# FFT-filter mixing and SwiGLU feed-forward on one core: the filter-half copies, the order and the engine split of the first sequence's prologue

## The chip, the cores and the metric

The kernel runs on one core of a Trainium2 chip. Times are device microseconds (us). "Span" is the time from the first to the last instruction of a profiled execution; it is about 1.8 us shorter than the time of the same run. I quote medians, and ratios with a 95% interval.

The engines are named as in the profile: PE is TensorE (matmuls), DVE is VectorE, ACT is ScalarE, POOL is GpSimd, SP is SyncE, whose queue issues DMAs here.

## The reference, cut to what matters

```python
# x: 8 sequences of 3008 x 256, filt_r and filt_i: 1505 x 256
Y = np.fft.rfft(x, axis=1) * (filt_r + 1j * filt_i)[None]
a = np.fft.irfft(Y, n=3008, axis=1).reshape(24064, 256)
xn = a / np.sqrt(np.mean(a * a, axis=-1, keepdims=True) + 1e-6) * rms_g
g = xn @ w_gate                                     # 256 -> 1536
out = (g / (1 + np.exp(-g)) * (xn @ w_val)) @ w_out # 1536 -> 256
```

The kernel does the transform as matmuls: a first DFT stage ("stage A", tile `pat`), transposes (`pt`), a second stage (the "products", tile `psb`, numbered 0 to 15), a multiplication with the filter, and the way back (`pgt`). Then come the norm and the feed-forward part, whose first matmul is the gate product `pg`.

## The kernel before

Sequence 0 has nothing to overlap with. It is done on chip in a prologue that ends with the first `pg` at about 50 us. After that, TensorE always has feed-forward work of one sequence to mix with the transform of the next.

A filter chunk is loaded into one half of 128 partitions and copied into the other half, because the multiplication needs the real part and the imaginary part on both halves. These are the parts that matter:

```python
def b_unit(b, i):                       # one product unit; b is the sequence
    ps = bank(3 if b else (0, 3, 4, 5)[i % 4], "psb")   # written out in two branches
    for u in range(2):
        ...
        nc.tensor.matmul(ps[:, u, :], w[:, k, :], t, start=True, stop=True)
    ...
    eng = nc.vector
    if (i in (5, 8, 11, 14)) if b else (i in (4, 8, 11)):
        eng = nc.gpsimd                 # ScalarE copies PSUM to v, GpSimd multiplies
        ...
        nc.scalar.activation(out=v, in_=ps, func=AXT.Copy)
    eng.tensor_tensor(out=s1, in0=ps, in1=f1, op=ALU.mult)
    eng.tensor_tensor(out=s2, in0=ps, in1=f2, op=ALU.mult)

def f_dup(c):                           # copy the halves of filter chunk c
    for t, a, e in ((fr[c], HALF, 0), (fi[c], 0, HALF)):
        if c == 2 or (c == 3 and a):
            nc.scalar.activation(out=t[a:a + HALF], in_=t[e:e + HALF], func=AXT.Copy)
        else:
            nc.gpsimd.tensor_copy(out=t[a:a + HALF], in_=t[e:e + HALF])
```

```python
# the prologue's program order, cut
for c in range(4):
    f_load(c, filt_r, fr[c], 0, nc.sync)
    if c < 3:
        f_load(c, filt_i, fi[c], HALF, nc.gpsimd)
nc.sync.dma_start(gsb, moe_rms_g...)    # the 256 gains, one per partition
...
for i in range(8):
    t1_unit(i)                          # transposes, and a copy by VectorE or ScalarE
f_dup(0); f_load(3, filt_i, ...); f_dup(1)
for i in range(16):
    if i == 7: f_dup(3)
    b_unit(0, i)
    if i % 2 and i >= 5: bit_unit(i - 5); bit_unit(i - 4)
    if i == 4: f_dup(2)
    if i == 11: w_load(0); w_load(1)    # the feed-forward weights
```

## Time and profile before

| | before |
|---|---|
| median of the first 3 runs | 904.32 us |
| profiled span | 903.3 us |
| TensorE busy | 878.7 us, 97% |
| last part of x on chip (last DMA engine) | 15.5 us |
| transposes start | 17.1 us |
| VectorE's filter products | 22.5 to 41.5 us |
| first gate product | 50.6 us |

The head of the profile's page gives the span, then busy time, share of the span and instruction count of each engine:

```profile
span 903.3 us, 17520 instructions
...
PE 878.7 (97%) x6329; PEld 561.0 (62%) x6329; DVE 676.9 (75%) x1075; ACT 619.3 (69%) x1047; POOL 391.4 (43%) x353
```

TensorE bounds the kernel as a whole, but it is not busy all through the prologue. The windows view shows this; each line is one stretch of the prologue, with busy time and instruction count of each engine, then the granted TensorE clock, the DMA share and GB/s:

```profile
core 0: us, PE busy (x) PEld busy (x) DVE busy (x) ACT busy (x) POOL busy (x), PEclk, DMA share, GB/s
...
17.00:34.00 17.00, 10.99 (x138) 8.54 (x139) 14.71 (x24) 11.07 (x13) 14.76 (x12) 0.96 0.62 138
34.00:44.00 10.00, 8.60 (x89) 7.54 (x89) 5.53 (x9) 5.60 (x13) 9.37 (x10) 0.55 0.30 48
44.00:52.00 8.00, 5.67 (x53) 3.82 (x53) 3.78 (x9) 3.67 (x7) 4.69 (x7) 0.87 1.20 174
```

From 17 to 34 us VectorE and GpSimd are the busiest engines. From 34 to 44 us TensorE seems to be, but at a granted clock of 0.55: it does little work in a lot of busy time.

VectorE's timeline over the products (start, duration, engine, line, operation, and in brackets the idle time before it and what ended that). Each multiplication takes about 0.68 us, and one follows the other every 0.6 us:

```profile
22.50 0.69 DVE L263 TENSOR_TENSOR ss<-psb,fr 128x512 f16<-128x512 f32 x1
...
32.92 0.68 DVE L264 TENSOR_TENSOR ss<-psb,fi 128x512 f16<-128x512 f32 x1
35.93 0.69 DVE L263 TENSOR_TENSOR ss<-psb,fr 128x512 f16<-128x512 f32 x1 [2.32 <-POOL ss L263]
...
40.80 0.68 DVE L264 TENSOR_TENSOR hh<-psb,fi 128x512 f16<-128x512 f32 x1
```

The stretch lasts 22.50 to 41.48, 19.0 us, and it has one hole of 2.32 us, which waits for a GpSimd product. GpSimd's timeline shows why: that product itself started late, since ScalarE had to bring it its copy `v` and was in two filter copies of 1.9 us:

```profile
34.61 1.26 POOL L263 TENSOR_TENSOR ss<-v,fr 128x512 f16<-128x512 f32 x1 [1.56 <-ACT v L261]
```

TensorE's timeline at the start of the prologue: stage A waits for x, then 64 transposes, then the products. The last line is the first gate product.

```profile
15.66 0.94 PE L486 MATMUL pat<-tb,xc 128*128 128x128 f16 x14 [0.76 <-DMA xc<-in_x_dram]
17.11 4.64 PE L509 MATMUL pt<-tb,aT 128*128 128x128 f16 x64 [0.51 <-ACT aT L492]
22.03 0.38 PE L241 MATMUL psb<-t,wbp 96*128 96x256 f16 x2 [0.28 <-DVE t L511]
...
50.59 1.06 PE L420 MATMUL pg<-xn,wg 128*128 128x512 f16 x2
```

### The profile page before, as it was taken

How to read it: one execution, taken by the hardware profiler on the slowest of the kernel's cores; microseconds unless marked ns; L12 is line 12 of the kernel's file. 1: busy time of each engine (PE TensorE's matmuls, PEld its weight loads, DVE VectorE, ACT ScalarE, POOL GpSimd, SP SyncE). 2: the span in 40 equal slices, each digit the busy share in tenths (PEclk: the TensorE clock that was granted, in tenths of full speed). 3: DMA queues.
4: the chain of work that ended last, by engine and by line, in shares of the span. 5: the costliest groups of instructions: out<-in, count | busy, mean ns of one | idle time of the engine just before them, and what ended most of it. 6: DMA issues, size and time to landing. Idle time of an engine off the chain costs nothing.

```text
span 903.3 us, 17520 instructions
## 1 busy us (share of the span) xinstructions
PE 878.7 (97%) x6329; PEld 561.0 (62%) x6329; DVE 676.9 (75%) x1075; ACT 619.3 (69%) x1047; POOL 391.4 (43%) x353
## 2 busy tenths in 40 slices
PE   8689999999999999999999999999999999999997
PEld 5565666666666666666666666666666666666564
DVE  7756767789887887888788886887878887555554
ACT  8657666677677766877667766787657765676443
POOL 7832740555635552465325552265514552043300
PEclk9799999999999999999999999999999999999999
DMA  9495734774664437444554347243252332321201
GB/s 199 82 182 159 144 76 164 166 171 79 165 168 116 90 72 213 106 95 113 135 147 111 88 96 193 81 105 82 74 173 71 65 88 54 97 70 48 60 24 46
DMA packets 79747, 100.91 MB, mean 112 GB/s; under 512 B 8097, under 2 KB 56417, under 8 KB 79277
## 3 DMA queue, kind: packets, MB, share of 16 engines
q1 hardware_dynamic: 69276, 83.45, 33.8%
q0 software_dynamic: 10384, 16.35, 11.4%
q8 instruction: 49, 0.80, 0.4%
q14 instruction: 38, 0.30, 0.1%
HBM read 67.67 MB, written 46.78 MB: 127 GB/s over the span
## 4 chain that ended last, share of the span: by engine, by line
PE 86%; issue 5%; DMA 3%; DVE 2%; POOL 2%; ACT 2%; SPq 0%; POOLq 0%; ACTq 0%
PE po L437 25%; PE pg L420 25%; PE pv L420 25%; PE psi L286 3%; PE psb L241 3%; PE psn L318 2%; DMA fr<-in_filt_r_dram 2%; PE psa L204 2%; PE psq L339 1%; DVE o L443 1%; DMA rb<-r_tmp 1%; POOL xc L189 0%; DVE hh L425 0%; ACT fr L478 0%; ACT sg L424 0%
## 5 line engine op out<-in xcount | busy, mean ns | idle before, releaser
L425 DVE TENSOR_TENSOR hh<-pv,sg 128x512 f16<-128x512 f32 (+1 forms) x576 | 391.4, 680 | 203.6 <-ACT sg L424 88.9
L424 ACT ACTIVATE sg<-pg 128x512 f16<-128x512 f32 (+1 forms) x576 | 338.8, 588 | 231.1 <-PE pg L420 223.1
L437 PE MATMUL po<-wo,hh 128*128 128x256 f16 x2256 | 342.3, 272 | 2.3 <-DVE o L443 1.6
L420 PE MATMUL pv<-xn,wv 128*128 128x512 f16 (+1 forms) x1152 | 337.9, 375 | 0.0
L420 PE MATMUL pg<-xn,wg 128*128 128x512 f16 (+1 forms) x1152 | 337.9, 375 | 0.0
L437 PEld LDWEIGHTS <-hh 128*128 128x128 f16 x2256 | 216.5, 98 | 99.2 <-issue 3.6
L277 POOL TENSOR_TENSOR s<-s,s 128x512 f16<-128x512 f16 x96 | 110.5, 1151 | 285.5 <-DVE s L271 199.5
L420 PEld LDWEIGHTS <-wv 128*128 128x128 f16 x1152 | 112.7, 98 | 131.2 <-issue 0.6
L403 POOL TENSOR_TENSOR xn<-y,rb 128x1024 f16<-128x1024 f32 (+1 forms) x45 | 126.1, 2802 | 46.7 <-DMA rb<-r_tmp 32.8
L420 PEld LDWEIGHTS <-wg 128*128 128x128 f16 x1152 | 109.2, 98 | 12.3 <-issue 0.3
L345 POOL TENSOR_TENSOR rho<-u,mhalf 128x4 f32<-128x4 f32 (+1 forms) x48 | 48.9, 1018 | 85.6 <-DVE u L343 85.6
L291 ACT ACTIVATE t<-psi 96x512 f16<-96x512 f32 x112 | 66.3, 592 | 11.8 <-PE psi L286 6.3
L324 ACT ACTIVATE y<-psn,gsb 128x512 f32<-128x512 f32 (+1 forms) x94 | 63.8, 678 | 10.1 <-PE psn L318 3.0
L271 DVE TENSOR_TENSOR s<-psb,fi 64x512 f16<-64x512 f32 x96 | 65.7, 684 | 3.0
L273 DVE SCALAR_TENSOR_TENSOR s<-psb,fi 64x512 f16<-64x512 f32 x96 | 66.5, 693 | 1.3
L247 DVE TENSOR_TENSOR s<-psb,fr 128x512 f16<-128x512 f32 x96 | 65.4, 681 | 0.0
L330 ACT ACTIVATE sq<-psn 128x512 f16<-128x512 f32 (+1 forms) x94 | 54.8, 583 | 0.0
L209 ACT ACTIVATE t<-psa 128x512 f16<-128x512 f32 x70 | 41.8, 597 | 5.6 <-PE psa L204 2.4
L286 PE MATMUL psi<-s,wi 128*128 128x256 f16 x248 | 45.4, 273 | 0.0
L241 PE MATMUL psb<-t,wb 96*128 96x256 f16 x224 | 43.0, 272 | 0.9 <-DVE s L264 0.9
L286 PEld LDWEIGHTS <-wi 128*128 128x128 f16 x248 | 24.2, 98 | 27.0 <-issue 1.9
L318 PEld LDWEIGHTS <-t 128*128 128x128 f16 x368 | 28.5, 99 | 19.9
(97 smaller groups left out, 515.7 us busy)
## 6 DMA issues: line engine op xcount, KB each, us to landing
out_dram<-o SPq DMA_DIRECT2D x84, 256.0 KB
xc<-in_x_dram POOLq DMA_DIRECT2D x56, 192.0 KB, 6.4
z_tmp<-t SPq DMA_DIRECT2D x28, 384.0 KB
t<-z_tmp SPq DMA_DIRECT2D x28, 384.0 KB
g_tmp<-t SPq DMA_DIRECT2D x56, 192.0 KB
rb<-r_tmp SPq DMA_DIRECT2D x41, 256.0 KB
t<-g_tmp SPq DMA_DIRECT2D x21, 384.0 KB
out_dram<-o SPq DMA_DIRECT2D x12, 192.0 KB
```

The source lines that it names most:

```text
L241: nc.tensor.matmul(ps[:, u, :], w[:, k, :], t, start=True, stop=True)
L247: nc.vector.tensor_tensor(out=s1, in0=ps, in1=f1, op=ALU.mult)
L271: nc.vector.tensor_tensor(out=s2[a], in0=ps[e], in1=f2[e], op=ALU.mult)
L273: nc.vector.scalar_tensor_tensor(out=s2[a], in0=ps[e], scalar=-1.0, in1=f2[e], op0=ALU.mult, op1=ALU.mult)
L277: nc.gpsimd.tensor_tensor(out=s, in0=s1, in1=s2, op=ALU.add)
L286: nc.tensor.matmul(ps[:, u, :], wi_at(q, 2 * i + u), ss[q][:, u, :], start=(q == 0), stop=(q == n - 1))
L291: nc.scalar.activation(out=st[b]["t3"][c][:, 2 * r:2 * r + 2, :], in_=ps[0:KR], func=AXT.Copy)
L403: nc.gpsimd.tensor_tensor(out=xv, in0=yv, in1=rv.unsqueeze(1).to_broadcast([P, 2, n, P]), op=ALU.mult)
L420: nc.tensor.matmul(ps[:, 0:w], wt[:, dt_, ts(jt, P)], xn[:, dt_, 0:w], start=(dt_ == 0), stop=(dt_ == 1))
L424: nc.scalar.activation(out=sg[:, 0:w], in_=pg[:, 0:w], func=AXT.Silu)
L425: nc.vector.tensor_tensor(out=hh[:, 0:w], in0=pv[:, 0:w], in1=sg[:, 0:w], op=ALU.mult)
L437: nc.tensor.matmul(po[s4 // 2][:, s4 % 2, :], hh[:, ts(s4, P)], wo[:, jt, :], start=(jt == 0 and s4 % 2 == 0), stop=(jt == JT - 1 and (s4 ...
```

## The change

The intent is to shorten VectorE's product stretch and to start it earlier. The filter halves are copied by three hands at once: ScalarE for most real halves, GpSimd for most imaginary ones, a DMA within the on-chip memory for one half. Products 0 to 3 are issued between the first transposes. GpSimd takes four product units instead of three. The load of the gains moves to the head of the SyncE queue, some small work moves between engines, and six warm-up matmuls fill the wait for x.

```diff
-        if (i in (5, 8, 11, 14)) if b else (i in (4, 8, 11)):
+        if (i in (5, 8, 11, 14)) if b else (i in (3, 7, 10, 13)):
# b_unit is split: b_mm issues the matmuls, b_unit can take its result
-    def f_dup(c):
+    def f_dup(c, which=(0, 1)):
+        for e in which:
+            t = (fr, fi)[e][c]
+            a, o = (0, HALF) if e else (HALF, 0)
+            if c == 3 and e == 0:
+                nc.sync.dma_start(t[a:a + HALF], t[o:o + HALF])
+            elif e and c < 3:
+                nc.gpsimd.tensor_copy(out=t[a:a + HALF], in_=t[o:o + HALF])
             else:
+                nc.scalar.activation(out=t[a:a + HALF], in_=t[o:o + HALF], func=AXT.Copy)
# y_first: the second half of the norm's multiply moves from VectorE to ScalarE
# t1_unit: transposes go to the PSUM pools pg and pv; ScalarE copies groups 1, 4 and 6 only
+        nc.sync.dma_start(gsb, moe_rms_g...)          # the gains, now before the filter
         for c in range(4):
             f_load(c, filt_r, fr[c], 0, nc.sync)
-            if c < 3:
-                f_load(c, filt_i, fi[c], HALF, nc.gpsimd)
-        nc.sync.dma_start(gsb, moe_rms_g...)
+            f_load(c, filt_i, fi[c], HALF, nc.gpsimd if c < 3 else nc.sync)
# stage A, before its fifth group:
+            if m == 4:
+                warm_up(6, 0)
-        for i in range(8):
-            t1_unit(i)
+        t1_unit(0)
         f_dup(0)
-        f_load(3, filt_i, fi[3], HALF, nc.gpsimd)
-        f_dup(1)
+        t1_unit(1)
+        ps0 = [b_mm(0, i) for i in range(4)]
+        t1_unit(2)
+        f_dup(3, (0,))
         for i in range(16):
-            b_unit(0, i)
+            b_unit(0, i, ps0[i] if i < 4 else None)
# t1_unit(3..7) and the other f_dup calls now follow units 0 to 10;
# w_load(0) and w_load(1) come after unit 13 instead of 11; t2_unit(2) copies on ScalarE
```

## The prediction

> What bounds the kernel now. Over the whole span the matmul engine is busy 878.7 of 903.3 us (page, part 1), and from 66 us on it is busy 97 to 99% of each stretch (windows view). Nothing in the change touches that part. The change works between 8 and 52 us, before the first gate product (timeline: pg at 50.8 us). A microsecond saved there should come off the end nearly one for one; far less than 2% (18 us) can be saved.
>
> How that prologue runs (timeline and landings in the trace):
> - DMA is saturated from 6 to 31 us. The last part of x lands at 15.5 us; filter chunk 0 at 18.5 (real) and 19.3 (imaginary); the last chunk at 28.8 and 31.0. The change does not lower these bytes (it adds 0.5 MB of copy), so the start of the transposes (17.1 us) stays.
> - VectorE then sets the pace: 13 product units of two 0.68 us multiplications (about 1.2 us a unit, pipelined), from 22.5 to 41.5 us. Pure work is 15.6 us; the main hole is 2.3 us at 33.6 (a wait for a GpSimd product that started late, at 34.6, since ScalarE was in 1.9 us filter copies).
> - TensorE is at half its clock from 32.8 to 43.0 us and from 49.9 to 53.3 (windows view by microsecond: 0.50). There a 96-wide product takes 0.08 instead of 0.043 us, and TensorE is the limit from 37 to 43 us.
>
> What the change does, costed:
> 1. Unit 3, 7, 10, 13 to GpSimd in place of 4, 8, 11: one unit less on VectorE, -1.2 us; the 2.3 us hole should mostly go, since GpSimd no longer copies the real halves (2 x 1.9 us) and ScalarE's imaginary-half copy moves behind the products' start.
> 2. First copies in parallel: real half of chunk 0 on ScalarE 18.6 to 20.5, imaginary on GpSimd 19.4 to 21.3 (before: ready at 22.5).
> 3. That gain is not collected: ScalarE's 1.0 us transpose copy of group 1 now stands behind its 1.9 us filter copy, so TensorE's products 2 and 3 wait until about 21.5, transposes of group 2 follow, and VectorE's copy of group 2 stands before product 0. I expect product 0 at about 23.4, later than before by about 1 us.
> 4. Sum for VectorE from 23.4: 12 x 1.2 + 3 x 0.6 = 16.2 us, plus about 1 us of holes: last product ends near 40.5 (before 41.5).
> 5. After it: one normalization multiply (0.75 us) and one transpose copy (0.4) leave VectorE's chain: 0.5 us saved before the first xn.
> 6. The memset and the six warm-up matmuls hide in the wait for x at 15.5.
>
> Clock: [...] TensorE's new hole at 19 to 21.5 may bring half clock early; fewer holes later may shorten the one at 33 to 43. This is worth 1 to 2 us either way.
>
> Predicted: first gate product at about 48.5 (before 50.8), time 902.0 us, 80% range 899.3 to 904.3. Faster by over 2%: 0.01; within: 0.985; slower: 0.005.
>
> Right if: chain has no 2.3 us GpSimd hole, product 0 starts near 23.4, first gate product comes 1 to 4 us earlier, stretch after it is as long as before. Wrong if: half clock covers 22 to 40 us, the DMA copy of chunk 3's real half lands after 36 us, or work after the prologue waits for x or weights, whose loads don't move.

The forecast came to 2.3 us, from 50.8 to 48.5 us for the first gate product and from 904.3 to 902.0 us in time. The "1 to 2 us either way" for the clock stands outside the sum; it was the author's estimate, and the text does not say from which numbers. What the text calls saturated DMA is a DMA share of 0.95 from 6 to 29 us in the windows view of the kernel before; from 29 to 30 us the share is 0.37, from 30 to 31 us nil.

## The result

| | before | after |
|---|---|---|
| median (4 runs each) | 904.31 us | 904.12 us (903.08 to 905.43) |
| ratio | 1 | 0.9998 (0.998 to 1.0015) |
| profiled span | 903.3 us | 902.2 us |

904.12 lies just within the predicted range, at its upper edge (904.3). The expected 2.3 us did not come: the medians differ by 0.2 us. A change worth nothing would have landed in the range too, so the hit by itself says little about the mechanism.

The head of the page after the change. Totals hardly move:

```profile
span 902.2 us, 17535 instructions
...
PE 875.6 (97%) x6335; PEld 559.0 (62%) x6335; DVE 672.9 (75%) x1070; ACT 622.7 (69%) x1051; POOL 390.3 (43%) x351
```

The windows view after, same stretches and columns as before:

```profile
17.00:34.00 17.00, 10.77 (x128) 9.49 (x128) 10.37 (x18) 10.61 (x10) 9.85 (x8) 0.90 0.77 167
34.00:44.00 10.00, 6.97 (x110) 5.80 (x110) 8.44 (x15) 8.52 (x18) 8.57 (x8) 1.00 0.08 16
44.00:52.00 8.00, 5.07 (x56) 3.46 (x54) 3.42 (x8) 5.16 (x10) 7.11 (x11) 1.00 1.07 158
```

VectorE has 4.3 us less work from 17 to 34 us (10.37 against 14.71) and 2.9 us more from 34 to 44. The clock is now 1.00 from 34 to 52 us, where it was 0.55 and 0.87.

VectorE's timeline after: the product stretch starts 3.7 us later than before, has no hole, and ends only 1.0 us later, at 42.44.

```profile
25.60 0.69 DVE L519 COPY t<-pt 96x1024 f16<-96x1024 f16 x1 [4.26 <-PE pt L517]
26.21 0.68 DVE L264 TENSOR_TENSOR ss<-psb,fr 128x512 f16<-128x512 f32 x1
...
41.76 0.68 DVE L265 TENSOR_TENSOR hh<-psb,fi 128x512 f16<-128x512 f32 x1
```

TensorE's timeline after shows two things that made the start late: x is waited for longer (1.62 us against 0.76), and products 2 and 3 wait 2.22 us for ScalarE's copy `t`.

```profile
18.09 0.94 PE L494 MATMUL pat<-tb,xc 128*128 128x128 f16 x14 [1.62 <-DMA xc<-in_x_dram]
19.54 1.60 PE L517 MATMUL pt<-tb,aT 128*128 128x128 f16 x16 [0.51 <-ACT aT L500]
21.40 0.60 PE L237 MATMUL psb<-t,wbp 96*128 96x256 f16 x4 [0.26 <-DVE t L519]
24.21 0.60 PE L237 MATMUL psb<-t,wbp 96*128 96x256 f16 x4 [2.22 <-ACT t L521]
...
51.05 0.38 PE L424 MATMUL pg<-xn,wg 128*128 128x512 f16 x1 [0.22 <-DVE xn L396]
```

ScalarE's timeline names the cause of the second: the copy `t` that TensorE needs stands behind the filter copy, which waits for the filter to land.

```profile
21.21 1.91 ACT L488 ACTIVATE fr<-fr 64x2048 f32<-64x2048 f32 x1 [1.73 <-DMA fr<-in_filt_r_dram]
23.14 1.02 ACT L521 ACTIVATE t<-pt 96x1024 f16<-96x1024 f16 x1
```

In this trace the first gate product comes at 51.05, not earlier than before (50.59). The span is 1.1 us shorter all the same.

### The profile page after: what moved, and what is told of

Read it like the earlier page. It is cut to its first block, busy times and chain, and to the rows that moved or that the text cites. A ratio compares the mean times of both kernels' runs of the same rounds, so it can differ in the third digit from the quotient of the medians.

```text
span 902.2 us, 17535 instructions
## 1 busy us (share of the span) xinstructions
PE 875.6 (97%) x6335; PEld 559.0 (62%) x6335; DVE 672.9 (75%) x1070; ACT 622.7 (69%) x1051; POOL 390.3 (43%) x351
## 4 chain that ended last, share of the span: by engine, by line
PE 87%; issue 5%; DVE 2%; DMA 2%; POOL 2%; ACT 1%; SPq 0%; DVEq 0%; POOLq 0%; ACTq 0%
PE po L441 25%; PE pg L424 25%; PE pv L424 25%; PE psb L237 3%; PE psi L287 3%; PE psn L319 2%; PE psa L204 2%; DMA fr<-in_filt_r_dram 1%; PE psq L340 1%; DVE o L447 1%; DMA rb<-r_tmp 1%; PE pt L517 0%; POOL xc L189 0%; DVE hh L429 0%; ACT sg L428 0%
## 5 line engine op out<-in xcount | busy, mean ns | idle before, releaser
L346 POOL TENSOR_TENSOR rho<-u,mhalf 128x4 f32<-128x4 f32 (+1 forms) x48 | 48.9, 1018 | 82.4 <-DVE u L344 82.4
```

## The experiments

The questions were these. Does the move of the gains delay x and the filter? Does the position of ScalarE's first filter copy cost the start? What does the clock do? And why does an earlier first gate product not shorten the time?

Twelve kernels were run, in three groups of four. Each group ran on one chip, and its four kernels share the runs of the before kernel. All were timed and all gave correct results. The before kernel's median in the three groups was 905.38, 905.55 and 905.98 us, with 11 runs each. It ranged from 903.9 to 908.1 us in the second group, so one run of one kernel says little about 1 us.

Three readings recur. "Landed" is when 15 of the 16 DMA engines had delivered x; this leaves out one slow engine. "Half clock" is a stretch in which the trace's clock records show a granted clock of 0.5. Half-clock time per run is worked out from the mean granted clock c and the span as 2·(1 − c)·span; figures for a kernel are means over its runs, since c is on record to 0.001, which is 1.8 us of half clock. The before kernel has 18.7 to 20.4 us of it in the three groups. In the fourteen traces 0.7 to 3.6 us of it lies at the very end of the span. The first 4 to 7 us of a trace have no clock record and count as full clock.

### e1: the changed kernel with the gains loaded late again

```diff
-        nc.sync.dma_start(gsb, moe_rms_g...)     # before the filter loads
         for c in range(4):
             f_load(...)
+        nc.sync.dma_start(gsb, moe_rms_g...)     # after them, as in the kernel before
```

> The changed kernel with the load of the 256 gains put back behind the filter loads. Theory A (the 4-byte packets of the gains at the head of the queue delay x and filter chunk 0): x is complete near 15.5 us instead of 17.95, real filter chunk 0 is ready near 18.7 instead of 21.1, product 0 starts near 23.7 instead of 26.2, and the time is about 2 us under the changed kernel (902). Theory B (the late x has another cause: the moved memset, the moved loads, or chance of that run): x still completes after 17 us, product 0 after 25.5, time within 0.7 us of the changed kernel.

Measured: median 906.70 us, ratio 1.0006 (0.9972 to 1.0039). x landed at 15.59 and real filter chunk 0 at 18.63, against 16.5 and 21.11 in the first trace of the changed kernel. The time did not improve. The trace of this run is spoiled for a direct comparison: the DFT tables landed 1.6 us late (8.56 instead of 7.0), and TensorE was at half clock from 9.0 to 19.3 us, so the transposes began only at 22.8. The timed runs are free of that choice of one trace, and they show no gain from this edit alone: theory A's 902 did not come.

### e2: the kernel before with the gains loaded first

```diff
+        nc.sync.dma_start(gsb, moe_rms_g...)
         for c in range(4):
             f_load(...)
-        nc.sync.dma_start(gsb, moe_rms_g...)
```

> The kernel before with nothing changed but the load of the gains moved to the head of the queue. Theory A: x completes near 17.5 to 18 us instead of 15.5, product 0 starts near 25 instead of 22.5, time 2 us over the kernel before (906.5). Theory B: x completes by 16.2 us, time within 0.7 us of the kernel before.

Measured: median 906.21 us, ratio 1.0008 (0.9977 to 1.0039). x landed at 16.25, against 15.0 in the kernel before. As in e1, half clock early on (9.9 to 20.2 us) spoiled the trace, and the DFT tables were late here too (8.39). The direction of the landing is as the theory of the gains says; no loss of time can be told from 1.

### e3: the changed kernel with the filter copy behind the second transposes

```diff
         t1_unit(0)
-        f_dup(0)
         t1_unit(1)
+        f_dup(0)
```

> The changed kernel with the transposes of group 1 and their ScalarE copy placed ahead of the ScalarE copy of filter chunk 0. Theory (the 1.0 us transpose copy behind the 1.9 us filter copy holds TensorE, and through the copy of group 2 VectorE's first product): the 2.2 us wait of the products for that copy vanishes, product 0 starts when the filter copy ends, near 23.2 instead of 26.2, VectorE's last product ends near 40 instead of 42.4, and the time falls by 1 to 2 us (less if GpSimd's last product, which ended at 42.9, then sets the end). Rival (the filter's arrival at 21.1 alone sets the start): product 0 moves by under 1 us, time within 0.5 us.

Measured: median 904.04 us, ratio 0.9976 (0.9946 to 1.0006). TensorE's timeline shows the wait gone, 0.16 us instead of 2.22:

```profile
21.35 1.01 PE L237 MATMUL psb<-t,wbp 96*128 96x256 f16 x4 [0.16 <-ACT t L521]
```

VectorE's first product started at 23.69 and the first gate product at 48.88, 2.2 us earlier than in the changed kernel's first trace. Against its second trace (e6 below: 24.26 and 48.47) the gate product is not earlier, so only the vanished wait is sure. The interval includes 1, so the gain in time is likely but not shown by this run alone.

### e4: both edits, e1 and e3

> Both edits: gains late, and group 1's transposes ahead of the filter copy. If both theories hold: x complete near 15.5, product 0 near 21.4, last product near 38 to 40, first gate product near 47.5 to 49 instead of 51, time 900 to 901.5. If only the copy order counts: about 902.5; if neither: about 904.

Measured: median 904.77 us, ratio 0.9985 (0.9954 to 1.0016); the 900 to 901.5 us expected if both theories hold did not come. TensorE's timeline shows the best start so far: a short wait for x, and none of note for ScalarE.

```profile
16.04 0.94 PE L494 MATMUL pat<-tb,xc 128*128 128x128 f16 x14 [0.32 <-DMA xc<-in_x_dram]
...
20.17 0.60 PE L237 MATMUL psb<-t,wbp 96*128 96x256 f16 x4 [0.23 <-ACT t L521]
```

The first VectorE product starts at 22.12 and the last ends at 38.35, 3.1 us earlier than in the kernel before (41.48). Yet the first gate product is at 48.87 and the span at 903.2. So 3 us in the middle of the prologue gave 1.7 us at its end and 0.1 us of span. The windows view of e4 shows where the first part went:

```profile
34.00:44.00 10.00, 7.80 (x87) 5.92 (x83) 5.33 (x10) 5.87 (x13) 8.63 (x10) 0.72 0.42 59
44.00:52.00 8.00, 6.75 (x49) 4.41 (x47) 3.44 (x8) 4.55 (x9) 5.90 (x9) 0.50 1.24 184
```

The granted clock is 0.50 for the whole stretch from 44 to 52 us, where the changed kernel had 1.00. TensorE was busy 6.75 us there with no more work. This made the clock a suspect in its own right.

### e5 and e6: both kernels again, unchanged

> The kernel before, unchanged, as a control with a trace of its own. Both theories: x complete by 16.2 us, real chunk 0 landed by 19 us, product 0 within 1 us of 22.5 unless the clock is halved early. It also shows whether the wait of 1.2 to 2.0 us for sequence 1's fourth chunk near 114 to 118 us, which the four experiments had and the first two traces had not, belongs to this chip or to the edits: if to the chip, it is here too.

> The changed kernel, unchanged, as a control. Gains theory: x complete at 16.5 to 18 us and real chunk 0 landed at 19.9 to 21.2, as in the three traces with the gains first; product 0 at 25 to 26.5; time within 1 us of the kernel before. If x completes by 16.2 here, its lateness was chance.

Measured: e5 (before) median 905.69 us, ratio 1.0005 (0.9983 to 1.0027); e6 (after) 905.21 us, ratio 0.9994 (0.9976 to 1.0012). These are the controls, and they taught the most about the first pair of traces. (As expected of e5, x was complete by 16.2 us there, at 15.72; e6 has it at 17.06.) TensorE's timeline of e6:

```profile
17.20 0.94 PE L494 MATMUL pat<-tb,xc 128*128 128x128 f16 x14 [1.16 <-DMA xc<-in_x_dram]
18.64 1.60 PE L517 MATMUL pt<-tb,aT 128*128 128x128 f16 x16 [0.51 <-ACT aT L500]
...
22.52 0.60 PE L237 MATMUL psb<-t,wbp 96*128 96x256 f16 x4 [1.40 <-ACT t L521]
...
48.47 1.19 PE L424 MATMUL pg<-xn,wg 128*128 128x512 f16 x2
...
114.87 0.38 PE L237 MATMUL psb<-t,wb 96*128 96x256 f16 x2 [1.48 <-ACT v L262]
```

VectorE's products run from 24.26 to 40.49, 16.2 us, exactly as long as in the first trace. But the start is 2 us earlier, and the first gate product is at 48.47, where the prediction put it (48.5). So part of the late start in the first trace belonged to that one execution: its last DMA engine delivered x 1.45 us after the fifteenth (17.95 against 16.5), in e6 0.55 us after it.

The last line above is new. TensorE waits 1.48 us near 113 us, long after the prologue, in sequence 1's product unit 12. The same chip ran e5 without this wait, so the chip alone does not make it. ScalarE's timeline takes it one step back: the copy `v` stands behind a copy `t`, whose buffer is still being stored.

```profile
113.74 0.59 ACT L292 ACTIVATE t<-psi 96x512 f16<-96x512 f32 x1 [2.11 <-DMA g_tmp<-t]
114.23 0.58 ACT L262 ACTIVATE v<-psb 128x512 f32<-128x512 f32 x1
```

### e7: the gains loaded four times at the head of the queue

```diff
+    more_g = [glob.tile([P, 2], FP32, name="more_g%d" % i) for i in range(3)]
-            nc.sync.dma_start(gsb, moe_rms_g...)
+            for dst in (gsb, *more_g):
+                nc.sync.dma_start(dst, moe_rms_g...)
```

> The changed kernel with the same 256 gains loaded four times at the head of the queue (three of them into tiles that nobody reads). Gains theory: each of these loads delays x by about 1 us, so x completes near 20 us, real chunk 0 lands near 23, product 0 starts near 28.5, and the time is 2.5 to 4 us over the changed kernel's. Rival (the packets are too small to matter; the lateness was chance): x and time as in the changed kernel, within 0.7 us.

Measured: median 908.52 us, ratio 1.003 (1.001 to 1.005), slower than 1 in the interval. But x did not land later: 15.43, earlier than with one load. The filter did start later: its first packets landed at 16.45 instead of about 14.3. So x is not held up in proportion to the number of these loads, and the theory "each such load delays x" falls in that form. The time was 3.3 us over e6's, as the theory had expected, but not by its route: the extra time came with a first gate product at 50.9 and a wait of 2.01 us of the kind seen in e6.

### e8: e4 with TensorE kept busier

```diff
# in b_mm: products of sequence 0 are computed twice, into the same place
-            nc.tensor.matmul(ps[:, u, :], w[:, k, :], t, start=True, stop=True)
+            for _ in range(1 if b else 2):
+                nc.tensor.matmul(ps[:, u, :], w[:, k, :], t, start=True, stop=True)
# in the tail of the prologue: ten more warm-up matmuls on zeros
+        warm_up(4, 0)
         q_unit(0, 0)
...
+        warm_up(6, 0)
         scale_apply(0, 0, 3)
```

> The kernel of the run with both edits (gains late, group 1 ahead of the filter copy) and, besides, TensorE kept busier in the prologue: every product of sequence 0 computed twice into the same place, and 10 more warm-up matmuls in the waits of the first norm. Clock theory (the 1.5 us that both edits gained up to 42 us were given back since the clock was at half from 38 to 52 us): no half clock between 20 and 50 us, first gate product near 47 us instead of 48.9, time 901 to 903, under both kernels. Rival (added matmuls only delay): first gate product at 49 or later, time 904.5 or more.

Measured: median 900.36 us, ratio 0.9937 (0.992 to 0.9955). This is the best version: its interval lies clear of 1 and clear of e6's, run on the same chip in the same rounds. Half-clock time over its runs fell to 3.6 us. The first gate product is at 48.00, where about 47 was expected. The expectation of no half clock between 20 and 50 us was missed in the trace: one stretch, 40.6 to 44.0 us, is left.

### e9: the kernel before with only these warm-up edits

> The kernel before with only the busier TensorE: each product of sequence 0 computed twice, and 10 more warm-up matmuls in the waits of the first norm. Clock theory (about 19 us at half clock in the kernel before cost it 2 to 4 us in the prologue): half clock falls under 8 us per run, time falls by 2 to 4 us, to 902 to 903.5. Rival (the gain of the best run so far came from the gains' place and the copy order, not from the clock): time within 1 us of the kernel before.

Measured: median 902.78 us, ratio 0.9965 (0.9941 to 0.9989). Half-clock time 3.9 us per run instead of 20.4; both figures are within what the clock theory expected. The windows view of e9 against that of the kernel before:

```profile
34.00:44.00 10.00, 7.59 (x112) 6.08 (x110) 5.95 (x10) 6.02 (x15) 9.38 (x10) 1.00 0.33 52
44.00:52.00 8.00, 7.27 (x64) 4.58 (x63) 4.38 (x10) 4.45 (x9) 5.89 (x9) 1.00 1.26 181
```

The clock is 1.00 in both stretches (0.55 and 0.87 before), and from 34 to 44 us TensorE is busy for less time (7.59 against 8.60) with more instructions (112 against 89). No part of the studied change is in this kernel, and it gains 3.2 us by the medians, more than the studied change was predicted to bring.

### e10: the changed kernel with the same warm-up edits

> The changed kernel with the same busier TensorE and nothing else. Clock theory: the changed kernel is at half clock for only 8 us a run, some 4 of them at the end, so there is little left to win: 0 to 1.5 us, time 903.5 to 905. Rival (the copy order and the gains' place are worth nothing, the busier TensorE is the whole of the best run's gain): time 900 to 901, as there.

Measured: median 903.21 us, ratio 0.9969 (0.9942 to 0.9995); half-clock time 6.6 us. e9 and e10 ran on the same chip in the same rounds. With the clock nearly equal, e10 shows no gain over e9 that can be measured: 903.21 against 902.78. The time is a little under the 903.5 to 905 expected by the clock theory and far from the rival's 900 to 901. No unmodified changed kernel ran in this group, so what the warm-up brought to the changed kernel was not measured; e11 below, in the same rounds and without the warm-up, has nearly the same ratio. The trace of e10 shows the first gate product at 50.71, against 48.66 in e9: VectorE's first product comes at 26.22. TensorE's hole behind ScalarE's filter copy is still there (1.62 us) and is followed by half clock from 22.9 to 26.3, and x was complete 1.5 us later than in e9 (16.73 against 15.21).

### e11 and e12: an earlier load, against the wait near 113 us

The theory was that the wait comes from loads and stores of sequence 1 that crowd together, and that one load issued two slots earlier would clear it. e11 is the changed kernel with this edit, e12 is e8 with it.

```diff
-                ... if c < 3 else b_at[4] + 1,
+                ... if c < 3 else b_at[4] + (-1 if b == 1 else 1),
                    t2_load, b, c)
```

> The changed kernel with sequence 1's fourth chunk loaded two steps earlier, ahead of a broadcast load in the same queue. Theory (part of the prologue's gain is given back near 113 us, where TensorE waits 1.5 us for a ScalarE copy that waits for the store of an earlier chunk, which was issued behind a load whose issue took 1.74 us instead of 0.38): that load is issued in 0.4 us, the wait near 113 us is gone, time about 1 us under the changed kernel. Rival: the stall belongs to the traffic of that moment; the wait stays between 110 and 120 us and the time within 0.5 us.

> The best run so far (gains late, group 1 ahead of the filter copy, busier TensorE) with the same earlier load. Its trace had no wait near 113 us, so by the give-back theory it gains 0 to 1 us on the mean: 899.5 to 900.5. If the earlier load hurts another transfer: 900.5 to 902.

Measured: e11 median 903.98 us, ratio 0.9974 (0.9952 to 0.9996); e12 900.82 us, ratio 0.9945 (0.9916 to 0.9974). e12 is no better than e8 and misses the 899.5 to 900.5 expected if the earlier load helped. e11's interval lies clear of 1, but with no unmodified changed kernel in its group this cannot be put down to the load. In e11 the wait is still there, as TensorE's timeline shows:

```profile
114.78 0.38 PE L237 MATMUL psb<-t,wb 96*128 96x256 f16 x2 [1.57 <-ACT v L262]
```

So the theory that this earlier load clears the wait falls. What is seen is that SyncE is slow to issue at that moment. Its timeline in e6 has one issue at 105.59 that takes 1.74 us, with the store behind it; in e10, which has no wait, the issue of the same load takes 0.39 us. First e6, then e10:

```profile
105.59 1.74 SPq L219 DMA_DIRECT2D t<-z_tmp  x1
107.43 0.48 SPq L295 DMA_DIRECT2D g_tmp<-t  x1
```

```profile
106.68 0.39 SPq L219 DMA_DIRECT2D t<-z_tmp  x1
107.17 0.48 SPq L296 DMA_DIRECT2D g_tmp<-t  x1
```

The store starts 1.84 us after the load's issue in e6 and 0.49 us in e10; the difference of 1.35 us is close to e6's wait of 1.48. In e11, where that load was issued earlier, it is the issue of the store itself that is slow:

```profile
106.71 1.03 SPq L295 DMA_DIRECT2D g_tmp<-t  x1
```

It took 1.03 us instead of 0.48, which is less than the wait of 1.57, so this accounts for a part only.

All seven traces with the wait (e1, e2, e3, e4, e6, e7, e11) also hold one DMA packet of the kind "instruction" (16 KB; in e2 8 KB) of 1.47 to 2.17 us that starts between 105.0 and 110.1 us. In the seven without it, the packets of this kind from 105 to 115 us take at most 0.97 us; the next of over 1.0 us (up to 1.40 us) come at 118 us or later. This is a coincidence seen 14 times of 14, not an experiment; I did not find a safe way to move that packet alone, and the cause stays open.

### The bookkeeping of all fourteen traces

The profiled span splits into the time until the first gate product ("prologue") and the rest. The rest, for the five traces that have neither the wait nor half clock just behind the prologue (after, e8, e9, e10, e12), is 851.2 to 851.9 us, mean 851.7. The last column is an estimate for each trace: 851.7, plus its wait, plus half of its half-clock time in the ten microseconds after the first gate product, where TensorE is taken to have enough work and to lose half of such time (in the kernel before, one pair of gate or value matmuls follows another after 0.86 us at half clock, from 50.59 us, and after 0.43 us at full clock, from 54.34 us).

| trace | VectorE's first product | prologue | wait near 115 us | half clock after it | rest | estimate of the rest |
|---|---|---|---|---|---|---|
| before | 22.5 | 50.6 | none | 2.7 | 852.7 | 853.0 |
| e5 before | 22.7 | 50.0 | none | 4.2 | 853.3 | 853.8 |
| after | 26.2 | 51.1 | none | none | 851.2 | 851.7 |
| e6 after | 24.3 | 48.5 | 1.48 | 2.6 | 853.9 | 854.5 |
| e1 | 27.5 | 52.6 | 1.81 | 4.2 | 854.9 | 855.6 |
| e2 | 26.8 | 52.3 | 2.03 | 2.0 | 855.2 | 854.7 |
| e3 | 23.7 | 48.9 | 1.21 | 1.1 | 853.4 | 853.5 |
| e4 | 22.1 | 48.9 | 1.84 | 3.2 | 854.3 | 855.1 |
| e7 | 25.3 | 50.9 | 2.01 | 3.5 | 855.4 | 855.5 |
| e8 | 22.7 | 48.0 | none | none | 851.9 | 851.7 |
| e9 | 22.4 | 48.7 | none | none | 851.6 | 851.7 |
| e10 | 26.2 | 50.7 | none | none | 851.8 | 851.7 |
| e11 | 24.5 | 49.2 | 1.57 | none | 852.6 | 853.3 |
| e12 | 22.5 | 47.8 | none | none | 851.8 | 851.7 |

The estimate meets the rest within 0.8 us in all fourteen, five of which set its 851.7. It leaves out one thing: e2 and e7 have a second half-clock stretch of 3.4 us behind the wait, from 119.1 and 119.3 us; with half of it added, the estimate would be 1.2 and 1.8 us too long there. So the bookkeeping fits the reading that the gains of the prologue do come off the end, and that a late start, half clock and the wait near 115 us take them back; it does not prove it. The times themselves point the same way for the clock: over the 109 timed runs with a clock on record, within one kernel of one group, a run with 1 us more half-clock time took 0.30 us longer (correlation 0.73); without the two slowest, both of the kernel before, it is 0.25 us (0.68). This is a correlation: a run that is late for another cause may leave TensorE idle, too. The experiment is e9: 16.5 us less half clock and 3.2 us less time, 0.19 us per us.

### Why the clock drops

Apart from the one at the kernel's end, half-clock stretches in these traces are 3.4, 6.8, 10.2 or 13.7 us long, multiples of 3.41. The clock records of the kernel before have 10.24 us at half clock (32.78 to 43.02), then 6.83 us at full clock, then 3.41 us at half clock (49.84 to 53.26). I therefore cut the traces into windows of 3.41 us, counted from such an edge. In the kernel before, the windows view shows the last two windows ahead of the drop at 32.8 us and the first one behind it:

```profile
25.98:29.39 3.41, 2.22 (x28) 1.22 (x24) 3.25 (x7) 2.80 (x2) 3.26 (x3) 1.00 0.81 154
29.39:32.80 3.41, 1.44 (x20) 1.21 (x21) 3.41 (x7) 3.39 (x4) 2.94 (x3) 1.00 0.03 6
32.80:36.21 3.41, 2.49 (x21) 1.80 (x20) 1.09 (x3) 3.39 (x9) 1.85 (x3) 0.50 0.00 0
```

TensorE was busy 1.44 of 3.41 us, 42%, and the next window was granted 0.50; after a window of 65% (2.22 of 3.41) the clock stayed at 1.00. The longest gap of TensorE that reaches into the window before the drop was 1.56 us, up to 30.83. The same cut of the changed kernel:

```profile
21.39:24.80 3.41, 1.18 (x11) 0.93 (x11) 0.00 (x0) 2.75 (x2) 2.17 (x2) 1.00 0.83 194
24.80:28.21 3.41, 3.41 (x36) 3.41 (x34) 2.61 (x5) 0.90 (x1) 1.34 (x1) 0.50 0.88 181
```

Here the change's own hole of 2.22 us (35% busy) is what precedes the drop, and most of the transposes that follow run at half clock (0.50 from 24.8 to 28.2 us): 48 of them take 4.54 us, against 64 in 4.64 before. The share does not decide alone: after a window of 50% (1.71 us at 46.4 to 49.8 us in the kernel before) and one of 53% (1.80 us at 37.2 to 40.6 us in e8) the next was granted 0.50, and after one of 64% (2.18 us at 35.0 to 38.4 us in e4) as well, but after another of 53% (1.82 us at 41.9 to 45.3 us in the changed kernel) it stayed at 1.00. Cut in this way up to 125 us, and counted from the clock and TensorE records, the fourteen traces have 6 windows at full clock with under 45% busy, and all 6 are followed by half clock; of 51 with 46 to 66%, 17 are; of 388 above that, none. These are counts of this kernel's runs; no limit follows from them. e9 is the experiment on this reading: only TensorE's activity was raised (from 29.4 to 32.8 us it is busy 1.95 us where it was 1.44), and the half clock at 32.8 to 43.0 and at 49.8 us was gone.

## Why the prediction was right or wrong

The prediction was right in "within 2%", and the time lay in its range (902.0 predicted, 904.12 measured, range to 904.3), but of the 2.3 us forecast 0.2 came. That the time still fell inside was in part luck: the late start and the gain from the clock, neither of them sized as they turned out, nearly cancelled, and the range reached to no change at all. It was right for several of its reasons, but not in all its steps; of its own "right if" conditions, the first pair of traces met only the vanished hole. The first two of its "wrong if" conditions did not come: half clock covered only 24.8 to 28.2 us, and chunk 3's DMA copy landed at 35.5 us (34.1 in e6).

1. **VectorE's stretch: right, to a tenth.** "12 x 1.2 + 3 x 0.6 = 16.2 us" was measured as 16.2 us in both traces of the changed kernel. The allowance "plus about 1 us of holes" was not needed. The 2.32 us hole vanished as predicted.

2. **The copy order: right in its mechanism, mis-sized in the first trace.** The prediction said that ScalarE's copy of group 1 behind its filter copy would make products 2 and 3 wait. They waited 2.22 us, and 1.40 us in e6. e3 and e4 moved that one call and the wait fell to 0.16 and 0.23 us. In place of "product 0 at about 23.4" the traces have 26.2 and 24.3.

3. **Failed step: "the change does not lower these bytes ..., so the start of the transposes (17.1 us) stays".** The amount of bytes was right and the conclusion was not: the transposes began at 19.5 and 18.6 us. The order of the loads had changed. Before, the load of the 256 gains was issued at 22.0 us, after, at 1.6. From 6 to 10 us, among the packets of x, the trace after has 274 packets of 4 bytes on the queue of the SyncE loads, 7 to 24 ns each; the trace before has 5. Of the fourteen traces, the six with one load of the gains at the head landed x on 15 engines at 16.07 to 16.51; six of the seven with it late at 14.81 to 15.59, and one (e8) at 16.14. So about 1 us of landing goes with this order; e2, where only the order was changed, agrees (16.25), with its late tables as a rival for a part. It is not a cost per load (e7, four loads, 15.43), and undoing it alone (e1) brought no time. The rest of the late start in the first trace came from one slow DMA engine in that execution, which e6 did not repeat.

4. **Failed step: a microsecond saved in the prologue "should come off the end nearly one for one".** e6 had the predicted prologue (first gate product at 48.47, 48.5 predicted, 1.5 to 2.1 us before the two traces of the kernel before), and its span was only 0.9 us shorter. The wait of 1.48 us near 113 us, absent in both traces of the kernel before, is enough for the 0.6 to 1.2 us that were missing. In the first pair it was the other way round: the prologue was 0.5 us longer and the rest about 1.6 us shorter; half clock, which ran on for 2.7 us into the feed-forward part before, no longer did (by the estimate above, worth about 1.3 us). "Stretch after it is as long as before" was wrong in both.

5. **Mis-sized term: the clock, "1 to 2 us either way".** The prediction saw the half clock in the kernel before and named its risk, but gave it no sign. The change halved it: 18.7 to 20.4 us per run before, 9.5 and 7.8 us after. At the 0.19 us per us of e9 to the 0.30 found within kernels this is an estimated gain of about 1.7 to 3.8 us, about as much as all else predicted together, and the measured time shows almost none of it. The late start and the wait are the losses that the traces show against it; that they spent it is argued from the bookkeeping, not shown. The warm-up alone was worth 3.2 us in the kernel before (e9).

6. **The tail: not separated.** "0.5 us saved before the first xn" fits the first pair: from VectorE's last product to the first gate product 9.1 us before and 8.6 after. In the second pair (e5, e6) both have 8.0. The clock differs in these stretches, so the term is neither confirmed nor refuted.

What became of the expected 2.3 us is therefore this. VectorE did lose 2.8 us of product stretch (19.0 to 16.2). A start 1.6 to 3.7 us later took it back. With the gain from the clock, the first trace ended 1.1 us of span ahead; the second had the better start, and a wait as large as what it lost. With the clock held up in both kernels, e9 and e10 differ by 0.4 us, in favour of the kernel before and within the noise.

Left open: how much of the changed kernel's time the warm-up recovers, since no group holds it with and without (e10 has no unmodified partner); why the versions with the gains late (e1, e4) had more half-clock time (17.5 and 14.4 us) than those with them first (9.5 and 7.8); what slows SyncE's issue and the store near 106 us; and whether e8's lead over e9 (ratios 0.9937 and 0.9965, in different groups, with overlapping intervals; e12 against e9 in the same rounds: 900.82 and 902.78) is the part of the change that works.

## What to carry to other kernels

When a prologue is reshuffled, cost three things beside the busiest engine's work: what now stands ahead of the first copy in each engine's queue (here a wait of 2.22 us), what now stands ahead of the first load in each DMA queue (here x landed about 1 us later), and how busy TensorE is (here 1.44 of 3.41 us came before 10.2 us at half clock). Duplicate work on an engine that would otherwise be idle was cheaper than idling here: with products computed twice and ten matmuls on zeros, the kernel before went from 905.98 to 902.78 us (e9). And repeat the unchanged kernels before explaining a difference of one or two microseconds: the second pair of traces overturned half of what the first pair suggested.
